# Tails of keys and queries loaded once per sequence, and the first sequence's query loads issued from ScalarE

## The chip, the cores and the metric

The kernel runs on one core of a Trainium2 chip. The metric is device time in microseconds; lower is better. The engines are named as in the profile: PE (TensorE, with PEld for its weight loads), DVE (VectorE), ACT (ScalarE), POOL (GpSimd) and SP (SyncE, which computes nothing here and issues DMAs). A row marked SPq or ACTq is the issue of a DMA on that engine's instruction stream.

## The reference, cut to what matters

Attention with a threshold over 4 sequences of 8 heads, 576 positions and 64 features, then two feed-forward layers on the result, all in float32:

```python
scores = q @ k^T / sqrt(64)                       # per sequence and head, 576 x 576
thresh = max(scores, -1) - tau
attn   = exp(where(scores >= thresh, scores, -1e9) - max)
attn   = attn / (sum(attn, -1) + 1e-9)
x      = (attn @ v) laid out as (4 * 576, 512)
x      = (h * clip(h + 3, 0, 6) / 6) @ w_out      # h = x @ w_in, 512 -> 2048 -> 512
x      = (max(h, 0) ** 2) @ w2_out                # h = x @ w2_in
```

## The kernel before, in words

A *unit* is a pair of heads of one sequence, so there are 16 units, 4 to a sequence (`u.b` is the sequence, `u.p` the pair, `u.i` the running number). 576 positions are 4 tiles of 128 (`NT = 4`) and a *tail* of 64. A unit has 9 *jobs*: 4 tiles of queries for each head and one job for the two tails together, so a sequence has 36 jobs. A job goes through the engines like this: `scores` on PE (name `s`), `soft1` and `soft2` on DVE, ACT and POOL (minimum `nm`, exponential, mask and sum, and a split into two halves of 16 bits, the last piece of which is line 281 on POOL, `gl` or `p`), then a transposing DMA issued by SP (line 283, `pt<-gl` in the first sequence, `pt<-p` later), and 5 jobs later (`LAG`) the product with the values on PE (`av`, line 305, name `o`). `finish` transposes a unit's result into `xh` and `xl`, the inputs of the first layer.

Before a unit's jobs, `prep_steps` transposes its keys and queries on PE (line 143, `tps`) and copies them on ACT. In the first sequence (`u.plain`) ACT alone copies; in later ones ACT and DVE split each value in two. The loads come two units ahead: in `run`, at a unit's jobs 2, 4 and 6 (`LOADS`), `load_qk` and `load_v` issue the loads for the unit after next. `kraw`, `qraw` and `vraw` have two buffers each. `load_qk` makes three DMAs for each of k and q: one for the four tiles, and one for each half of the partitions that brings the 64 tail rows of both heads of the pair.

The layers' weights come as 64-bit floats. Each of 64 weight tiles is loaded (`wd`, 512 KB), turned to 32 bits (lines 478 to 487, `wc` and `wraw`), split into two parts (lines 506 and 507) and written to DRAM (`scr`, line 490), from where the later sequences read it. Three `wd` tiles are in flight at most (`NWD`). The first tile is asked for after job 14 (`FIRST_W`). `hidden` (line 547, `hp`) and `output` (line 581, `y`) are the layers' matmuls; the steps of the next sequence's attention are put between them.

The order of instructions on each engine is not that of the code: a scheduler of the framework lists them by its own estimate of when each is ready. Each engine then runs its list strictly in order, and SP's list holds nearly all loads, all transposing DMAs and all writes.

Of the kernel before, what the change touches and what calls it, by code (L numbers as in the profile page):

```python
# [10 lines left out]
F32 = mybir.dt.float32  # L11
# [21 lines left out]
def attention_moe_moe_kernel(  # L33
# [12 lines left out]
    nc = tc.nc  # L46
    B, H, S, D = q.shape
    DM = out.shape[1]
    DFF = moe_w_in.shape[1]
    P = 128  # L50
    NT = S // P
    TAIL = S - NT * P
    assert TAIL * 2 == P and D * 2 == P
    NPAIR = H // 2
# [10 lines left out]
    ld = ctx.enter_context(tc.tile_pool(name="ld", bufs=1))  # L65
# [9 lines left out]
    ident = const.tile([P, P], F32, name="ident")  # L75
# [12 lines left out]
    own = [slice(0, D), slice(D, 2 * D)]  # L88
# [28 lines left out]
    class Unit:  # L117
        pass

    def load_qk(u, nm, eng=nc.sync):  # L120
        src = k if nm == "k" else q
        t = ld.tile([P, NT + 1, 2, D], F32, name=f"{nm}raw", bufs=2)
        pr = src[u.b, 2 * u.p:2 * u.p + 2]
        eng.dma_start(out=t[:, 0:NT], in_=pr[:, 0:NT * P, :].rearrange("h (p t) d -> p t h d", t=NT))

        for o in own:
            eng.dma_start(out=t[o, NT], in_=pr[:, NT * P:, :].rearrange("h p d -> p h d"))
        setattr(u, nm, t)

    def load_v(u):  # L130
        u.v = t = ld.tile([P, 2, NT + 1, D], F32, name="vraw", bufs=2)
        pr = v[u.b, 2 * u.p:2 * u.p + 2]
        nc.sync.dma_start(out=t[:, :, 0:NT, :], in_=pr[:, 0:NT * P, :].rearrange("h (p t) d -> p h t d", t=NT))
        for o in own:
            nc.sync.dma_start(out=t[o, :, NT, :], in_=pr[:, NT * P:, :].rearrange("h p d -> p h d"))

    def transpose_part(t, part, wide=False):
        if wide:
            a = ps_s.tile([P, 2, 512], F32, tag="s", name="tps")[:, 0]
        else:  # L140
            a = ps_a.tile([P, 512], F32, tag="acc", name="tps")
        for i, j in enumerate((0, 1) if part == 0 else (2, 3, 4)):
            nc.tensor.transpose(a[:, i * P:i * P + P], t[:, j].rearrange("p h d -> p (h d)"), ident)  # L143
        return a

    def cols(part):
        return (0, QA) if part == 0 else (QA, QB)

    def prep_steps(u):

        u.plain = u.b == 0
        if u.plain:

            u.qf = q_pl[:, u.i % 2]
            u.kf = xr[u.i % 2]
            for part in (0, 1):
                a = transpose_part(u.k, part, u.i == NPAIR)
                c0, n = cols(part)
                nc.scalar.activation(out=u.kf[:, c0:c0 + n], in_=a[:, 0:n], func=AF.Copy)
                yield  # L160
            for part in (0, 1):
                a = transpose_part(u.q, part, u.i == NPAIR)
                c0, n = cols(part)
                for h in range(2):
                    qf = u.qf[own[h], h * NT + 2 * part:h * NT + 2 * part + 2, :]
                    nc.scalar.activation(out=qf, in_=a[own[h], 0:2 * P].rearrange("p (t c) -> p t c", t=2), func=AF.Copy, scale=qs[own[h]])
                    if n > 2 * P:
                        nc.scalar.activation(out=u.qf[own[h], 2 * NT, own[h]], in_=a[own[h], 2 * P:n], func=AF.Copy, scale=qs[own[h]])
                yield
            yield from prep_v(u)  # L170
            return
        u.qs = [q_st[h][u.i % 2] for h in range(2)]
        u.ks = [k_st[h][u.i % 2] for h in range(2)]
        for part in (0, 1):
            a = transpose_part(u.k, part, u.i == NPAIR)
            c0, n = cols(part)
            for h in range(2):
                kh = u.ks[h][own[h], 0, c0:c0 + n]
                nc.scalar.activation(out=kh, in_=a[own[h], 0:n], func=AF.Copy)
                nc.vector.tensor_tensor(out=u.ks[h][own[h], 1, c0:c0 + n], in0=a[own[h], 0:n], in1=kh.bitcast(F32), op=ALU.subtract)  # L180
            yield
        for part in (0, 1):
            a = transpose_part(u.q, part, u.i == NPAIR)
            c0, n = cols(part)
            for h in range(2):
                for a0, d0, m in ((0, c0, 2 * P), (2 * P, NT * P + 64, n - 2 * P)):
                    if m > 0:
                        qh = u.qs[h][own[h], d0:d0 + m]
                        nc.scalar.activation(out=qh, in_=a[own[h], a0:a0 + m], func=AF.Copy, scale=qs[own[h]])
                        nc.vector.scalar_tensor_tensor(out=u.qs[h][own[1 - h], d0:d0 + m], in0=a[own[h], a0:a0 + m], scalar=qs[own[h]], in1=qh.bitcast(F32), op0=ALU.mult, op1=ALU.subtract)  # L190
            yield
        for h in range(2):
            nc.sync.dma_start(out=u.ks[h][own[1 - h], 0, :].bitcast(F32), in_=u.ks[h][own[h], 0, :].bitcast(F32))
        yield from prep_v(u)

    def prep_v(u):

        vin = u.v.rearrange("p h t d -> p (h t d)")
        am = st.tile([P, 1], F32, name="am", bufs=2)
        nc.vector.tensor_reduce(out=am, in_=vin, axis=AX.X, op=ALU.max, apply_absolute_value=True)  # L200
        a = ps_a.tile([P, 512], F32, tag="acc", name="vm")
        nc.tensor.matmul(a[:, 0:P], lhsT=am.to_broadcast([P, P]), rhs=ident, start=True, stop=True)
        u.vsc = sc = st.tile([P, 1], F32, name="vsc", bufs=2)
        nc.vector.tensor_reduce(out=sc, in_=a[:, 0:P], axis=AX.X, op=ALU.max)
        yield
        nc.vector.tensor_scalar(out=sc, in0=sc, scalar1=2.0 ** -100, scalar2=2.0 ** -13, op0=ALU.max, op1=ALU.mult)
        nc.vector.reciprocal(out=sc, in_=sc)
        nc.vector.tensor_scalar(out=sc.bitcast(I32), in0=sc.bitcast(I32), scalar1=0x7f800000, scalar2=None, op0=ALU.bitwise_and)
        v16 = at.tile([P, 2, 2, NT + 1, D], F16, name="v16")
        u.v1, u.v2 = v16[:, 0], v16[:, 1]  # L210
        v1 = u.v1.rearrange("p h t d -> p (h t d)")
        v2 = u.v2.rearrange("p h t d -> p (h t d)")
        if u.b < 2:
            nc.scalar.activation(out=v1, in_=vin, func=AF.Copy, scale=sc)
            nc.vector.scalar_tensor_tensor(out=v2, in0=vin, scalar=sc, in1=v1, op0=ALU.mult, op1=ALU.subtract)
        else:
            nc.scalar.activation(out=vin, in_=vin, func=AF.Copy, scale=sc)
            nc.scalar.activation(out=v1, in_=vin, func=AF.Copy)
            nc.gpsimd.tensor_tensor(out=v2, in0=vin, in1=v1, op=ALU.subtract)
# [152 lines left out]
    def run(us, all_jobs, pr):  # L372
        n = len(all_jobs)
        for i in range(n + LAG):
            if i < n:
                j = all_jobs[i]
                if j.first:
                    if pr is not None:
                        for _ in pr:
                            pass  # L380
                    pr = prep_steps(us[j.u.i + 1]) if j.u.i + 1 < len(us) else None
                scores(j)
                soft1(j)
            if i >= 1 and i - 1 < n:
                soft2(all_jobs[i - 1])
                jj = all_jobs[i - 1]
                if jj.hd == "t":
                    recips(jj.u, 2 * NT, 1)
                elif jj.t % 2:
                    recips(jj.u, jj.hd * NT + jj.t - 1, 2)  # L390
            x = i - LAG
            if 0 <= x < n:
                j = all_jobs[x]
                if j.hd == "t" or j.u.b == 0:
                    av([j])
                elif j.t % 2:
                    av([all_jobs[x - 1], j])
                if j.hd == 1 and j.t % 2:
                    finish(j.u, j.t // 2)
            if i < n and pr is not None:  # L400
                if next(pr, 1) == 1:
                    pr = None
            if i < n and all_jobs[i].u.i + 2 < len(us):
                nu = us[all_jobs[i].u.i + 2]
                if all_jobs[i].n == LOADS[0]:
                    load_qk(nu, "k")
                if all_jobs[i].n == LOADS[1]:
                    load_qk(nu, "q")
                if all_jobs[i].n == LOADS[2]:
                    load_v(nu)  # L410
            yield (i, n)
        return pr
# [285 lines left out]
```

## Time and profile before

| | us |
|---|---|
| three timed runs | 1114.97, 1115.55, 1117.37 (median 1115.55) |
| profiled execution | 1115.3, of which the span of the instructions is 1113.5 |
| PE busy | 1054.3 (95%) |
| ACT, DVE, POOL busy | 731.5, 721.4, 591.9 |
| share of the chain that ended last on PE | 68% |

The span is cut into stretches in the rows below. The first sequence's attention fills the first 100 us, the weight tiles are converted from 53.6 to 353.1 us, and after 400 us PE is busy nearly without a gap. Busy times of PE are modelled at their ends, so a busy PE may still be short of its peak.

### The profile page before, as it was taken

What the parts mean: (1) busy time and instruction counts of PE and PEld (TensorE: products, weight loads), DVE (VectorE), ACT (ScalarE), POOL (GpSimd) and SP (SyncE); (2) the same over time, 40 slices, a digit from 0 to 9 for tenths busy, and PEclk for the clock granted to TensorE, in tenths of its full rate; (3) what the DMA queues carried; (4) which work ended last, traced back from release to release, by engine and by line L of the source; (5) the groups of instructions that cost most, each with busy time, mean ns of one, the idle gap of its engine ahead of it and who ended that gap; (6) DMA issues with size and microseconds to landing.
All of it is one profiled execution on the core that took longest, in us unless ns stands there. A gap on an engine that the chain in (4) does not pass through costs nothing.

```text
span 1113.5 us, 24082 instructions
## 1 busy us (share of the span) xinstructions
PE 1054.3 (95%) x9136; PEld 1018.6 (91%) x9136; DVE 721.4 (65%) x1306; ACT 731.5 (66%) x1384; POOL 591.9 (53%) x654
## 2 busy tenths in 40 slices
PE   6777899999899999999999999999999999999998
PEld 4556789988888999999999999999999999999998
DVE  5798678887787756767666656767656343435342
ACT  6887778788787757667775657757765445435432
POOL 5786678878679744456544454445643232214221
PEclk9989999999999999999999999999999999999999
DMA  6898999999998565556754545446544243323221
GB/s 143 181 234 183 268 237 274 267 248 271 256 266 203 136 154 139 133 123 133 152 125 125 130 135 127 103 125 120 119 111 110 85 118 80 94 77 86 77 67 43
DMA packets 291267, 168.70 MB, mean 152 GB/s; under 512 B 223824, under 2 KB 252496, under 8 KB 291152
## 3 DMA queue, kind: packets, MB, share of 16 engines
q1 hardware_dynamic: 289824, 166.84, 61.5%
q8 instruction: 72, 1.18, 0.5%
q10 hardware_dynamic: 1328, 0.33, 0.1%
q14 instruction: 43, 0.35, 0.1%
HBM read 99.62 MB, written 21.50 MB: 109 GB/s over the span
## 4 chain that ended last, share of the span: by engine, by line
PE 68%; DVE 2%; ACT 2%; POOL 1%; DMA 1%; issue 1%; SPq 0%; DVEq 0%; POOLq 0%; ACTq 0%
PE y L581 30%; PE hp L547 28%; PE s L250 4%; PE o L305 3%; PE tps L143 1%; PE ot L608 1%; DMA wd<-in_moe_w_out_dram 0%; DMA wd<-in_moe_w_in_dram 0%; DVE wc L481 0%; PE xT L322 0%; DVE wraw L482 0%; POOL gl L561 0%; POOL xl L337 0%; DVE wraw L487 0%; DVE ya L587 0%
## 5 line engine op out<-in xcount | busy, mean ns | idle before, releaser
L561 POOL TENSOR_TENSOR gl<-g,gh 128x576 fp32r<-128x576 f32 x128 | 193.8, 1516 | 257.3 <-ACT gh L560 253.5
L581 PE MATMUL y<-gh,who 128*128 128x288 f32 x1024 | 225.3, 301 | 8.3 <-DVE e L273 4.7
L547 PE MATMUL hp<-xh,whi 128*128 128x288 f32 x1024 | 224.8, 301 | 7.4 <-DVE g L558 2.7
L581 PE MATMUL y<-gh,wlo 128*128 128x288 f32 x1024 | 220.6, 296 | 0.0
L581 PE MATMUL y<-gl,who 128*128 128x288 f32 x1024 | 219.0, 297 | 0.3 <-POOL gl L561 0.2
L547 PE MATMUL hp<-xh,wli 128*128 128x288 f32 x1024 | 219.0, 296 | 0.0
L547 PE MATMUL hp<-xl,whi 128*128 128x288 f32 x1024 | 218.7, 295 | 0.0
L581 PEld LDWEIGHTS y<-gh,who 128*128 128x128 f32 x1024 | 163.9, 189 | 10.3 <-issue 2.7
L547 PEld LDWEIGHTS hp<-xh,whi 128*128 128x128 f32 x1024 | 163.6, 189 | 9.3 <-DVE e L273 2.4
L581 PEld LDWEIGHTS y<-gh,wlo 128*128 128x128 f32 x1024 | 164.9, 189 | 0.0
L547 PEld LDWEIGHTS hp<-xh,wli 128*128 128x128 f32 x1024 | 164.8, 189 | 0.0
L547 PEld LDWEIGHTS hp<-xl,whi 128*128 128x128 f32 x1024 | 164.6, 189 | 0.0
L581 PEld LDWEIGHTS y<-gl,who 128*128 128x128 f32 x1024 | 163.8, 189 | 0.7 <-POOL gl L561 0.7
L256 DVE TENSOR_REDUCE nm<-s 128x1 f32<-128x576 f32 x144 | 107.9, 751 | 36.8 <-PE s L250 29.1
L281 POOL TENSOR_TENSOR p<-e,p 128x512 f16<-128x512 f32 x108 | 130.8, 1211 | 0.0
L587 DVE TENSOR_TENSOR ya<-y,ya 128x576 f32<-128x576 f32 (+1 forms) x97 | 71.6, 748 | 77.2 <-PE y L581 76.6
L506 ACT ACTIVATE who<-wraw 128x512 fp32r<-128x512 f32 x128 | 79.4, 628 | 63.2 <-PE y L581 37.5
L273 DVE SCALAR_TENSOR_TENSOR e<-s,thr,e 128x576 f32<-128x576 f32 x108 | 88.0, 815 | 42.0 <-ACT e L266 41.3
L305 PE MATMUL o<-v,pt 128*128 128x64 f16 (+1 forms) x2016 | 93.0, 198 | 17.7 <-DMA pt<-gl 10.9
L507 DVE TENSOR_TENSOR wlo<-wraw,who 128x512 fp32r<-128x512 f32 x96 | 80.5, 846 | 43.4 <-ACT who L506 41.1
L305 PEld LDWEIGHTS <-pt 128*128 128x128 f16 x2016 | 74.6, 99 | 33.2 <-DMA pt<-gl 13.9
L279 ACT ACTIVATE p<-e 128x576 f16<-128x576 f32 x108 | 73.4, 680 | 36.7 <-DVE e L273 35.2
(92 smaller groups left out, 1700.5 us busy)
## 6 DMA issues: line engine op xcount, KB each, us to landing
wraw<-scr SPq DMA_DIRECT2D x192, 256.0 KB, 2.7
wd<-in_moe_w_in_dram SPq DMA_DIRECT2D x32, 512.0 KB, 5.0
scr<-wraw SPq DMA_DIRECT2D x64, 256.0 KB, 4.0
wd<-in_moe_w_out_dram SPq DMA_DIRECT2D x32, 512.0 KB, 5.5
kraw<-in_k_dram SPq DMA_DIRECT2D x16, 256.0 KB, 4.1
vraw<-in_v_dram SPq DMA_DIRECT2D x16, 256.0 KB, 3.3
out_dram<-wd SPq DMA_DIRECT2D x16, 256.0 KB, 2.8
qraw<-in_q_dram SPq DMA_DIRECT2D x15, 256.0 KB, 3.8
```

The lines of the kernel that those rows point to most:

```text
L250: nc.tensor.matmul(s[:, half, 0:HALF], lhsT=u.qs[sl][:, cs], rhs=u.ks[sl][:, kk, c], start=i == 0, stop=i == len(ops) - 1)
L256: nc.vector.tensor_reduce(out=j.nm, in_=j.s, axis=AX.XY, op=ALU.min)
L273: nc.vector.scalar_tensor_tensor(out=j.e, in0=j.s, scalar=j.thr, in1=j.e, op0=ALU.is_le, op1=ALU.mult, accum_out=u.sm[:, col:col + 1])
L279: nc.scalar.activation(out=p16[:, 0:S], in_=e, func=AF.Copy)
L281: nc.gpsimd.tensor_tensor(out=p16[:, S + TAIL:], in0=e[:, 0:NT * P], in1=p16[:, 0:NT * P], op=ALU.subtract)
L305: nc.tensor.matmul(o[:, n * w:n * w + w], lhsT=j.pt[:, c, :], rhs=vv[:, hs, vc, :], start=i == 0, stop=i == len(ops) - 1)
L506: nc.scalar.activation(out=h, in_=t, func=AF.Copy)
L507: (nc.gpsimd if fresh else nc.vector).tensor_tensor(out=l, in0=t, in1=h.bitcast(F32), op=ALU.subtract)
L547: nc.tensor.matmul(hp[:, a, 0:HALF], lhsT=w[:, cs], rhs=x[c][:, a * HALF:(a + 1) * HALF], start=i == 0, stop=i == 3 * NC - 1)
L561: nc.gpsimd.tensor_tensor(out=gl, in0=gf, in1=gh.bitcast(F32), op=ALU.subtract)
L581: nc.tensor.matmul(a[:, k_, 0:HALF], lhsT=w_hl[wuse[(tag, "o", f)]][w][:, cs], rhs=g[f][:, k_ * HALF:(k_ + 1) * HALF], start=i == 0, stop= ...
L587: nc.vector.tensor_tensor(out=y, in0=av_, in1=y, op=ALU.add)
```

## The change

`load_qk` no longer loads tails. A new function, `load_tails`, loads the tails of all 8 heads of a sequence into one tile (`ktail`, `qtail`, one buffer each) with two DMAs, one for each half of the partitions. It is called when the first unit of a sequence is loaded. `transpose_part` takes the fifth 128-column piece from that tile instead of from `kraw` or `qraw`, which shrink from five tiles to four. And in `run`, as long as the job at hand belongs to the first sequence, the queries of the unit after next are loaded through ACT's queue.

```diff
+    def load_tails(b, nm, eng=nc.sync):
+        t = ld.tile([P, H, D], F32, name=f"{nm}tail", bufs=1)
+        for o in own:
+            eng.dma_start(out=t[o], in_=(k if nm == "k" else q)[b, :, NT * P:, :].rearrange("h p d -> p h d"))
+        tails[nm] = t
+
+    tails = {}
+
     def load_qk(u, nm, eng=nc.sync):
         src = k if nm == "k" else q
-        t = ld.tile([P, NT + 1, 2, D], F32, name=f"{nm}raw", bufs=2)
+        t = ld.tile([P, NT, 2, D], F32, name=f"{nm}raw", bufs=2)
         pr = src[u.b, 2 * u.p:2 * u.p + 2]
-        eng.dma_start(out=t[:, 0:NT], in_=pr[:, 0:NT * P, :].rearrange("h (p t) d -> p t h d", t=NT))
-
-        for o in own:
-            eng.dma_start(out=t[o, NT], in_=pr[:, NT * P:, :].rearrange("h p d -> p h d"))
+        eng.dma_start(out=t, in_=pr[:, 0:NT * P, :].rearrange("h (p t) d -> p t h d", t=NT))
+        if u.p == 0:
+            load_tails(u.b, nm, eng)
         setattr(u, nm, t)
+        setattr(u, nm + "t", tails[nm])
...
-            nc.tensor.transpose(a[:, i * P:i * P + P], t[:, j].rearrange("p h d -> p (h d)"), ident)
+            x = tail[:, 2 * u.p:2 * u.p + 2] if j == NT else t[:, j]
+            nc.tensor.transpose(a[:, i * P:i * P + P], x.rearrange("p h d -> p (h d)"), ident)
...
+                eng = nc.scalar if all_jobs[i].u.b == 0 else nc.sync
                 if all_jobs[i].n == LOADS[0]:
                     load_qk(nu, "k")
                 if all_jobs[i].n == LOADS[1]:
-                    load_qk(nu, "q")
+                    load_qk(nu, "q", eng)
```

With other loads to place, the scheduler lists the rest anew as well. Three places follow; line numbers in the changed kernel are 12 to 14 higher behind the new function, so that 295 there is the transposing DMA of line 283 here.

On SP, where the first weight tiles are loaded. Before, this is behind the thirteenth transposing DMA of the kernel (the second row here):

```order
L127 DMA qraw<-in_q_dram 64x2x64 x2
L283 DMA_TRANSPOSE pt<-gl 128x9x128
L463 DMA wd<-in_moe_w_in_dram 128x4x256 x3
L283 DMA_TRANSPOSE pt<-gl 128x9x128 x2
L490 DMA scr_681<-wraw 128x512
L463 DMA wd<-in_moe_w_in_dram 128x4x256
L133 DMA vraw<-in_v_dram 128x2x256
L135 DMA vraw<-in_v_dram 64x2x64 x2
```

In the changed kernel it is ahead of the first transposing DMA:

```order
L134 DMA kraw<-in_k_dram 128x8x64
L477 DMA wd<-in_moe_w_in_dram 128x4x256 x3
L134 DMA kraw<-in_k_dram 128x8x64
L295 DMA_TRANSPOSE pt<-gl 128x9x128 x5
L143 DMA vraw<-in_v_dram 128x2x256
L145 DMA vraw<-in_v_dram 64x2x64
```

So the first three weight loads moved from behind 13 transposing DMAs to ahead of all of them, and the write of the first converted tile (`scr`), which stood ahead of the sixteenth, now stands behind the sixth.

On SP, at the end of the first sequence. Before, all 36 of its transposing DMAs (the last five are in the third and sixth row) come ahead of the next `w_out` tiles:

```order
L124 DMA qraw<-in_q_dram 128x8x64
L127 DMA qraw<-in_q_dram 64x2x64 x2
L283 DMA_TRANSPOSE pt<-gl 128x9x128 x2
L133 DMA vraw<-in_v_dram 128x2x256
L135 DMA vraw<-in_v_dram 64x2x64 x2
L283 DMA_TRANSPOSE pt<-gl 128x9x128 x3
L490 DMA scr_1757<-wraw 128x512
L465 DMA wd<-in_moe_w_out_dram 128x1024
L283 DMA_TRANSPOSE pt<-p_1810 128x9x128
L490 DMA scr_1829<-wraw 128x512
L465 DMA wd<-in_moe_w_out_dram 128x1024
```

In the changed kernel:

```order
L295 DMA_TRANSPOSE pt<-gl 128x9x128 x2
L479 DMA wd<-in_moe_w_out_dram 128x1024
L504 DMA scr_1817<-wraw 128x512
L479 DMA wd<-in_moe_w_out_dram 128x1024
L134 DMA kraw<-in_k_dram 128x8x64
L504 DMA scr_1891<-wraw 128x512
L479 DMA wd<-in_moe_w_out_dram 128x1024
L134 DMA qraw<-in_q_dram 128x8x64
L295 DMA_TRANSPOSE pt<-gl 128x9x128 x5
```

Three weight loads, two writes and the loads of a later unit's keys and queries moved ahead of the last five transposing DMAs of the first sequence.

On ACT, during the jobs of the first sequence's third unit, where the fourth unit's queries are copied (`ya`) and the second unit's result is written (`xh_104`). Before:

```order
L266 ACTIVATE gh<-s,nm 128x576
L166 ACTIVATE ya<-tps,qs 64x256
L329 ACTIVATE xh_104<-xT 64x64
L168 ACTIVATE ya<-tps,qs 64x64
L166 ACTIVATE ya<-tps,qs 64x256
L279 ACTIVATE gl<-gh 128x576
```

In the changed kernel:

```order
L278 ACTIVATE gh<-s,nm 128x576
L324 ACTIVATE os<-o,sm 128x64
L291 ACTIVATE gl<-gh 128x576
L341 ACTIVATE xh_104<-xT 64x64
L134 DMA qraw<-in_q_dram 128x8x64
L178 ACTIVATE ya<-tps,qs 64x256
L180 ACTIVATE ya<-tps,qs 64x64
L125 DMA qtail<-in_q_dram 64x8x64 x2
```

The load of a coming unit's queries stands directly ahead of two of those copies, and the two query tail loads of the second sequence follow them; none of the three stood on ACT before.

## Rows read from the trace of the kernel before

**Rows 1.** Busy time and instructions of each engine by stretch, granted clock, DMA share, GB/s.

```profile
0.00:10.00 10.00, 4.03 (x13) 2.91 (x14) 1.31 (x5) 4.02 (x9) 5.78 (x22) 1.00 0.60 143
10.00:60.00 50.00, 37.53 (x310) 27.95 (x309) 40.63 (x97) 40.47 (x82) 34.27 (x68) 0.95 0.82 171
60.00:100.00 40.00, 30.95 (x306) 22.99 (x304) 36.69 (x86) 36.38 (x81) 33.05 (x58) 0.93 0.99 218
100.00:110.00 10.00, 8.39 (x102) 7.91 (x100) 6.80 (x16) 6.90 (x16) 6.75 (x10) 1.00 0.86 172
110.00:120.00 10.00, 5.61 (x70) 5.02 (x71) 3.34 (x10) 4.06 (x11) 2.48 (x4) 0.99 1.06 251
120.00:400.00 280.00, 260.81 (x2258) 251.72 (x2257) 220.50 (x379) 225.96 (x433) 217.34 (x202) 0.99 0.94 238
400.00:1113.00 713.00, 706.99 (x6087) 700.12 (x6085) 412.15 (x718) 413.72 (x756) 292.28 (x293) 1.00 0.46 111
```

**Rows 2.** Waits of PE from 10 to 100 us: total, times, longest.

```profile
PE o L305 <- DMA pt<-gl: 8.4, 5, 3.9
```

**Rows 3.** Timeline of SP's issues: start, duration, instructions.

```profile
49.23 1.68 SPq L463 DMA_DIRECT2D wd<-in_moe_w_in_dram  x3
51.11 5.51 SPq L283 DMA_TRANSPOSE pt<-gl  x2
57.60 0.35 SPq L490 DMA_DIRECT2D scr<-wraw  x1
...
60.52 1.61 SPq L283 DMA_TRANSPOSE pt<-gl  x1
...
64.78 7.82 SPq L283 DMA_TRANSPOSE pt<-gl  x4
```

**Rows 4.** Timeline of POOL: the last pieces of jobs 16 and 18.

```profile
51.84 1.17 POOL L281 TENSOR_TENSOR gl<-gh,gl 128x512 f16<-128x512 f32 x1
...
55.88 1.15 POOL L281 TENSOR_TENSOR gl<-gh,gl 128x512 f16<-128x512 f32 x1
```

**Rows 5.** Timeline of PE; in brackets the idle time before, and its end.

```profile
58.37 1.67 PE L305 MATMUL o<-v,pt 128*128 128x128 f16 x14 [3.92 <-DMA pt<-gl]
```

**Rows 6.** Timeline: DMA issues of queries and tails on ACT, of tails on SP.

```profile
0.74 0.71 ACTq L124 DMA_DIRECT2D qraw<-in_q_dram  x1
1.49 1.38 ACTq L127 DMA_DIRECT2D qraw<-in_q_dram  x2
...
73.34 1.35 SPq L127 DMA_DIRECT2D kraw<-in_k_dram  x2
```

**Rows 7.** Timeline of the start: tail transpose on PE, then DVE.

```profile
6.87 0.42 PE L143 MATMUL tps<-ident,kraw 128*128 128x128 f32 x1
...
8.00 0.82 DVE L200 TENSOR_REDUCE am<-vraw 128x1 f32<-128x640 f32 x1 [0.87 <-DMA vraw<-in_v_dram]
...
10.81 0.76 DVE L256 TENSOR_REDUCE nm<-s 128x1 f32<-128x576 f32 x1 [1.99 <-PE s L246]
```

**Rows 8.** Timeline of ACT past 60 us: weight conversions (first, last) and a split.

```profile
62.82 0.66 ACT L478 ACTIVATE wc<-wd 128x512 f32<-128x512 f32 x1
63.38 0.62 ACT L506 ACTIVATE whi<-wraw 128x512 fp32r<-128x512 f32 x1
...
69.64 0.68 ACT L478 ACTIVATE wc<-wd 128x512 f32<-128x512 f32 x1 [0.37 <-DMA wd<-in_moe_w_out_dram]
```

**Rows 9.** Timeline of all engines where the first sequence ends.

```profile
106.38 4.66 SPq L283 DMA_TRANSPOSE pt<-gl  x3
...
111.03 0.58 PE L305 MATMUL o<-v,pt 128*128 128x64 f16 x14 [2.43 <-DMA pt<-gl]
...
111.73 0.45 SPq L465 DMA_DIRECT2D wd<-in_moe_w_out_dram  x1
...
116.63 0.66 ACT L478 ACTIVATE wc<-wd 128x512 f32<-128x512 f32 x1 [1.84 <-DMA wd<-in_moe_w_out_dram]
```

**Rows 10.** DMA issues: count, KB each, median us from issue to landing.

```profile
wd<-in_moe_w_out_dram SPq DMA_DIRECT2D x32, 512.0 KB, 5.5
```

More of the change, by code (lines that the diff above doesn't have):

```diff
@@ L135, in load_v, with transpose_part @@
             nc.sync.dma_start(out=t[o, :, NT, :], in_=pr[:, NT * P:, :].rearrange("h p d -> p h d"))
-    def transpose_part(t, part, wide=False):
+    def transpose_part(u, nm, part, wide=False):
+        t, tail = getattr(u, nm), getattr(u, nm + "t")
         if wide:
@@ L156, in prep_steps @@
             for part in (0, 1):
-                a = transpose_part(u.k, part, u.i == NPAIR)
+                a = transpose_part(u, "k", part, u.i == NPAIR)
                 c0, n = cols(part)
@@ L161, in prep_steps @@
             for part in (0, 1):
-                a = transpose_part(u.q, part, u.i == NPAIR)
+                a = transpose_part(u, "q", part, u.i == NPAIR)
                 c0, n = cols(part)
@@ L174, in prep_steps @@
         for part in (0, 1):
-            a = transpose_part(u.k, part, u.i == NPAIR)
+            a = transpose_part(u, "k", part, u.i == NPAIR)
             c0, n = cols(part)
@@ L182, in prep_steps @@
         for part in (0, 1):
-            a = transpose_part(u.q, part, u.i == NPAIR)
+            a = transpose_part(u, "q", part, u.i == NPAIR)
             c0, n = cols(part)
```

## The prediction

> **What bounds the kernel now.** I read the stretches first [rows 1]. From 400 us on PE is busy 706.99 of 713 us: nothing that SP or ACT do there can matter. From 120 to 400 it is idle 19.2 of 280. What is left lies in front: PE's idle time is 12.5 us from 10 to 60, 9.1 from 60 to 100, 6.0 from 100 to 120. So the time after 120 us is a block of PE work that moves as a whole, and the question is when the first sequence's attention hands it over. In that attention PE is not the bound: from 60 to 100 us DVE is busy 36.69 and ACT 36.38 of 40 us, but from 10 to 60 only 40.63 and 40.47 of 50, so 9.4 and 9.5 us are idle there, and from 100 to 120 they do 10.1 and 11.0 us of work in 20 [rows 1].
>
> Why there is idle time in the middle I read from PE's waits: between 10 and 100 us it stood 8.4 us before value products for a transposed tile [rows 2]. The largest of these, 3.92 us, ends at 58.37 [rows 5]. SP's issues say where it is from [rows 3]: three weight loads of 512 KB go out at 49.23, then two transposing DMAs take 5.51 us to issue, where three take 4.66 at 106.38 [rows 9], then SP waits for the first converted weight tile, which it has to write at 57.60. Only then, at 60.52, goes the transposing DMA of job 16, whose data POOL had finished at 51.84 + 1.17 = 53.01 [rows 4]. It is 7.5 us late. Those of jobs 17 and 18 come after 64.78, and job 18's data were ready at 55.88 + 1.15 = 57.03: at least 7.7 us late. These DMAs waited for SP's order, not for their data.
>
> **The change, part by part.**
>
> *Start.* The four tail DMAs in front carry 512 KB in all instead of 128 KB, so 393,216 more bytes lie ahead of the first values and the next keys. At the first stretch's 143 GB/s that is 2.7 us [rows 1]; it is the upper end. The lower is 0: the first values' reduction on DVE ends at 8.82, and DVE then idles 1.99 us until the first scores [rows 7]; the key tail is transposed at 6.87 [rows 7], behind other transposes. The tails are the nearer of the two, since the first scores need them whole. I take +1.0.
>
> *SP.* Before, it issues twelve key tails (two for each of units 0 to 5), ten query tails and five query loads during the first sequence; now four key tails and one query load. That is 22 issues less; at 1.35/2 = 0.68 us each [rows 6] 14.9 us of SP's time. None of it counts by itself; it counts where a transposing DMA stands behind it. What the scheduler makes of the room counts more: the three weight loads go ahead of the first transposing DMA instead of behind the thirteenth, and the first converted tile's write stands behind the sixth, with the conversion on DVE's list ahead of that job's own mask. So the pile-up at 49 to 66 us is gone. I count the wait of 3.92 [rows 5] as saved: −3.9. Upper end 0: the first value products, which follow three 512 KB loads instead, may wait as long. Lower end −9.4, all of DVE's idle time from 10 to 60 [rows 1]. I stay with the one wait, because the first product comes five jobs behind its DMA and has slack that a product in mid-stream has not.
>
> *ACT.* Four query loads and two tail loads are new on its list; an issue there takes 0.71 and 1.38/2 = 0.69 us [rows 6], 4.1 us in all, during which ACT computes nothing. Do they also wait? Each stands ahead of copies that wait for the very transposes that free its buffer, so no. Queued behind each are those copies, then the next job's exponential, for which DVE waits. By their places, two of the four query loads come in the first 20 us and one before 60, where ACT has 9.5 us to spare; the rest, one query load and two tails, fall where ACT is busy 91%: 3 × 0.69 = +2.1. Against that, three conversions and two splits of weights that ran on ACT from 62.8 to 70 us now come earlier: 3 × 0.66 + 2 × 0.62 = 3.2 us [rows 8]. Together −1.1; ends −3.2 (the issues all hidden) and +4.1 (no slack used).
>
> The page "DMA: Bandwidth & Descriptors" of the Trainium skill says (section "Issuing engines are not separate DMA queues") that DMAs from several engines run on the same 16 DMA engines and only the issuing sequencer's time is saved. By it the move to ACT's queue brings no bandwidth and is worth 0 unless SP's order holds something up; the pile-up above says it does, so I weigh it as a rival below.
>
> *End of the first sequence.* Now PE waits 2.43 us for a transposed tile at 111.03, ACT 1.84 us for the next `w_out` tile at 116.63, since that was issued only at 111.73, behind the transposing DMAs of 106.38 [rows 9]. In the changed order three such tiles go ahead of the last five transposing DMAs. I count ACT's wait as gone and PE's as left: −1.8. The lower end is −6.0, all of PE's idle time there; the upper is the slow rival below.
>
> *Later.* In the later sequences' loads 40 tail issues become 8, and the PE's transposes read as many columns as before, from another tile. From 120 to 400 us PE idles 19.2 us for many reasons [rows 1]; the new order may win or lose some of it. The one-buffer tails must wait for the last unit's transposes, which stand on PE about where SP comes to them. I take 0, from −4 to +4, a fifth of that idle time.
>
> *Sum.* 1.0 − 3.9 − 1.1 − 1.8 = −5.8. The profiled execution took 1115.3 us (span 1113.5 and 1.8 around it), which is the median of the timed runs, 1115.55, but for 0.25. So 1115.3 − 5.8 = **1109.5**.
>
> **The rivals.**
>
> *Slower: the weights get in front of the last transposes.* Ahead of the first sequence's last five transposing DMAs stand three weight loads, two writes and two loads: 3 × 512 + 4 × 256 KB = 2.62 MB, which at the 251 GB/s of 110 to 120 us is 10.4 us of transfers [rows 1]. On PE, 40 matmuls stand between the last scores of the sequence and the first of these five products; at 706.99/6087 = 0.116 us each [rows 1] they cover 4.6 us, and 5.8 are left. Besides, on ACT the conversion of the first of these weight tiles now stands ahead of the last three jobs' exponentials: if it waits for the whole landing, 5.5 us [rows 10], they do too. That is +11.3, and with the terms ahead of it (+1.0 − 3.9 − 1.1) 1115.3 + 7.3 = 1122.6. It decides from the point where those transposes land 4 us or more later than PE comes to them, which takes up what the middle won. For it speaks that two transposing DMAs took 5.51 us to issue behind three such loads [rows 3]; against it, that the five become ready one after the other, 2.8 us apart (36 jobs in the first 100 us), so that only the first ones meet the full queue, and that the same bytes then no longer hold up the conversions that follow.
>
> *No change: SP's lateness is cover.* The transposed tiles are used five jobs later, and DVE and ACT are busy 92% from 60 to 100 us; if they are the true bound, what is gained before 60 us is spent waiting later, and the new issues on ACT eat the rest. Time 1115.3, the sum with all terms 0. For it: of the 8.4 us that PE waited, all is before an engine that is itself not the bound. Against it: DVE and ACT idle 9.4 us just there. The rule of the Trainium skill named above leads to this case too.
>
> *More: the hand-over comes earlier and everything keeps pace.* If all of the idle time from 10 to 60 on DVE goes and PE's 6.0 from 100 to 120 too: 1115.3 + 1.0 − 9.4 − 1.1 − 6.0 = 1099.8.
>
> **How the numbers follow.** A measurement of this kernel can tell about 0.2%, 2.2 us, from no change. Forecast (1104 to 1113): 0.52. More, below 1104: 0.12. No change (1113.3 to 1117.8): 0.17. Slower, the first rival or a smaller share of it: 0.19, of which about 0.09 above 1120. The likeliest is the forecast, 1109.5. With 0.07 left below 1102 and 0.09 above 1120 the range is 1102 to 1120; the forecast's own range is 1104 to 1113. Faster by over 0.2%: 0.64; same 0.17; slower 0.19.
>
> **What the profile will show.** If the steps hold: PE has no wait of 3 us or more for a transposed tile between 40 and 70 us; the transposing DMAs of jobs 16 to 18 go within 2 us of their data; DVE and ACT are busier from 20 to 50 us and less from 60 to 100; the queries' issues on ACT take 0.7 us each with no wait ahead; PE is busy over 15 of the 20 us from 100 to 120; and past 400 us nothing differs but the shift. The start is wrong if the first scores come over 2 us later. The prediction fails if the last five transposed tiles of the first sequence, or the first ones behind the early weight loads, hold PE for 4 us or more, or if the shift at 120 us is lost again by 400.

## The result, and the profile after

The changed kernel takes 1129.63 us (median of 4, 1129.14 to 1130.04) against 1115.38 for the kernel before on the same chip: ratio 1.0119, 95% interval 1.0094 to 1.0144. It is 14 us slower, outside the range given. Its profiled execution took 1129.9 us, with a span of 1128.0.

The stretches of [rows 1] in the changed kernel (busy time and instructions of PE, PEld, DVE, ACT, POOL; granted clock; DMA share; GB/s), the last one up to its end:

```profile
0.00:10.00 10.00, 3.56 (x12) 2.38 (x13) 1.31 (x5) 2.92 (x5) 5.77 (x22) 1.00 0.83 187
10.00:60.00 50.00, 36.54 (x272) 26.21 (x271) 44.04 (x94) 40.91 (x84) 36.93 (x64) 0.90 0.93 208
60.00:100.00 40.00, 30.83 (x337) 24.27 (x333) 32.37 (x78) 31.78 (x75) 27.15 (x52) 0.91 0.93 182
100.00:120.00 20.00, 14.45 (x135) 12.13 (x132) 14.95 (x33) 13.50 (x28) 13.68 (x21) 0.91 1.02 212
120.00:400.00 280.00, 253.57 (x2213) 244.35 (x2213) 212.94 (x369) 219.85 (x427) 207.35 (x198) 0.98 0.88 230
400.00:1128.00 728.00, 720.27 (x6185) 712.94 (x6183) 420.26 (x731) 420.65 (x769) 300.34 (x300) 1.00 0.46 111
```

From 10 to 60 us DVE does 44.04 us of work instead of 40.63, as forecast; from 60 to 100 it does 4.3 us less and ACT 4.6. But PE, which did 260.81 us of work from 120 to 400, now does 253.57. Over the span PE is busy 1059.2 us with the same 9136 matmuls (1054.3 before), and idle 1128.0 − 1059.2 = 68.8 instead of 59.2. So of the 14.5 us of span 9.6 are idle time of PE and 4.9 are matmuls that ran longer; the granted clock is 0.986 over the span against 0.992.

Four checkpoints, read from the timelines, say where the time went: the minimum of job 28 on DVE (the first of the sequence's last unit) and of job 36 (its last job), and the first and the 32nd finished hidden tile (`gh<-g` on ACT; the 32nd is the last of the first sequence's second layer). From there to the last hidden tile both kernels take 707.7 to 707.9 us.

| us | job 28 | job 36 | first hidden tile | 32nd hidden tile | between the tiles |
|---|---|---|---|---|---|
| before | 76.7 | 98.4 | 126.6 | 387.7 | 261.1 |
| changed | 76.1 | 108.8 | 134.3 | 402.0 | 267.7 |
| difference | −0.6 | +10.4 | +7.7 | +14.3 | +6.6 |

At job 28 nothing is lost. 8.3 us are lost from there to the first hidden tile and 6.6 in the 260 us after it. Of the 6.6, 3.8 are idle time of PE (21.8 us between the two tiles against 18.0) and 2.8 matmuls that ran longer (245.8 us busy against 243.1).

What PE waits for between 10 and 100 us in the changed kernel (total, times, longest); it answers to [rows 2]:

```profile
PE s L258 <- DVE gh L285: 12.2, 7, 3.0
...
PE o L317 <- DMA pt<-gl: 1.1, 1, 1.1
```

The waits of scores for masks before:

```profile
PE s L246 <- DVE gh L273: 4.3, 4, 2.0
```

The 8.4 us of waits for transposed tiles are down to 1.1; scores wait for DVE's masks instead, 12.2 us against 4.3. DVE between 25 and 33 us (start, duration; in brackets, in later rows, the idle time before):

```profile
25.39 1.37 DVE L495 TENSOR_SCALAR wc<-wc 128x512 int32<-128x512 int32 x1
26.68 0.81 DVE L285 SCALAR_TENSOR_TENSOR gh<-s,thr,gh 128x576 f32<-128x576 f32 x1
...
27.83 1.64 DVE L496 SCALAR_TENSOR_TENSOR wraw<-wd,wc 128x512 int32<-128x512 int32 x1
...
31.20 0.74 DVE L268 TENSOR_REDUCE nm<-s 128x1 f32<-128x576 f32 x1
...
32.60 1.72 DVE L496 SCALAR_TENSOR_TENSOR wraw<-wd,wc 128x512 int32<-128x512 int32 x1
```

Conversions of the early weight tiles stand between the first masks and minima. Job 10's minimum comes at 34.9 us instead of 30.5; by job 28 that is made up.

SP does what the order said: three weight loads ahead of the first transposing DMAs, and the sequence's last five behind three more, issued from 101.48 us on. These rows answer to [rows 3, 9]:

```profile
10.99 2.39 SPq L477 DMA_DIRECT2D wd<-in_moe_w_in_dram  x3
...
17.88 12.82 SPq L295 DMA_TRANSPOSE pt<-gl  x5
...
106.78 12.85 SPq L295 DMA_TRANSPOSE pt<-gl  x5
```

Around 82 us, on DVE and on PE:

```profile
82.03 0.82 DVE L212 TENSOR_REDUCE am<-vraw 128x1 f32<-128x640 f32 x1 [3.29 <-DMA vraw<-in_v_dram]
...
83.73 2.26 PE L258 MATMUL s<-xr,ya 128*128 128x288 f32 x4 [3.04 <-DVE gh L285]
```

`am<-vraw` is the reduction of the values of the *second* sequence's first unit. It stands ahead of the masks of jobs 27 to 31 of the *first*, and they wait with it. At the sequence's end DVE, ACT and PE show the same thing with weights (DVE's rows first, then ACT, DVE, PE):

```profile
106.14 1.69 DVE L227 SCALAR_TENSOR_TENSOR v<-vraw,vsc,v 128x640 f16<-128x640 f32 x1
...
110.16 0.68 DVE L496 SCALAR_TENSOR_TENSOR wraw<-wd,wc 128x512 int32<-128x512 int32 x1
...
111.50 1.42 DVE L495 TENSOR_SCALAR wc<-wc 128x512 int32<-128x512 int32 x1
...
124.77 0.66 ACT L492 ACTIVATE wc<-wd 128x512 f32<-128x512 f32 x1 [2.20 <-DMA wd<-in_moe_w_in_dram]
...
125.97 0.62 ACT L341 ACTIVATE xh<-xT 64x64 fp32r<-64x64 f32 x2
...
127.77 0.41 DVE L342 TENSOR_TENSOR xl<-xT,xh 128x256 fp32r<-128x256 f32 x1
...
126.58 0.41 PE L155 MATMUL tps<-ident,kraw 128*128 128x128 f32 x2 [1.78 <-DVE xl L342]
```

A value split of the second sequence (1.69) and two conversions stand ahead of and among the last three masks, and the last results `xh`, `xl`, which the first layer needs, come behind a conversion that waits 2.20 us for its load.

### The profile page after: what moved, and what is told of

The parts are those of the page before. It is cut to its first block, busy times and chain, and to the rows that moved or that the text cites. A ratio compares the mean times of both kernels' runs of the same rounds, so it can differ in the third digit from the quotient of the medians.

```text
span 1128.0 us, 24031 instructions
## 1 busy us (share of the span) xinstructions
PE 1059.2 (94%) x9136; PEld 1022.3 (91%) x9136; DVE 725.9 (64%) x1306; ACT 729.6 (65%) x1384; POOL 591.2 (52%) x654
## 4 chain that ended last, share of the span: by engine, by line
PE 72%; DVE 8%; ACT 7%; DMA 7%; issue 3%; POOL 2%; SPq 1%; DVEq 0%; ACTq 0%; POOLq 0%
PE y L595 31%; PE hp L561 29%; PE s L262 4%; PE o L317 4%; DMA wd<-in_moe_w_in_dram 3%; DMA wd<-in_moe_w_out_dram 2%; PE s L258 2%; DVE wraw L496 1%; DVE nm L268 1%; DMA vraw<-in_v_dram 1%; ACT wc L492 1%; DVE gh L285 1%; PE tps L155 1%; DVE wraw L501 1%; PE ot L622 1%
## 5 line engine op out<-in xcount | busy, mean ns | idle before, releaser
L561 PEld LDWEIGHTS hp<-xh,whi 128*128 128x128 f32 x1024 | 164.1, 190 | 12.2 <-issue 6.3
L317 PEld LDWEIGHTS <-pt 128*128 128x128 f16 x2016 | 76.8, 100 | 27.0 <-issue 9.5
```

Source lines behind the costliest of these rows:

```text
L317: nc.tensor.matmul(o[:, n * w:n * w + w], lhsT=j.pt[:, c, :], rhs=vv[:, hs, vc, :], start=i == 0, stop=i == len(ops) - 1)
L561: nc.tensor.matmul(hp[:, a, 0:HALF], lhsT=w[:, cs], rhs=x[c][:, a * HALF:(a + 1) * HALF], start=i == 0, stop=i == 3 * NC - 1)
```

## The experiments

Behind each kernel stands its ratio to the kernel before, run on the same chip, with the 95% interval; 1.001 is 1.1 us. No edit changes what is computed. The gates below add a dependence by one more small operation on POOL, whose output is overwritten; but with each the scheduler lists everything anew, so that no edit moves one instruction alone.

**Halves of the change, and the early weights.** Three theories at first: E, the early conversions of the first weight tiles cost the time; A, the query issues on ACT do; T, the bulk of tails does. `e1_tails_only` puts the query loads back on SP:

```diff
-                    load_qk(nu, "q", eng)
+                    load_qk(nu, "q")
```

> The changed kernel with all query loads back on SP; the tails still come once per sequence. Theory E (early weights: the first three conversions stand on DVE and ACT among the masks of the first jobs, where DVE has no room): here too the first conversion stands behind the fourth mask, so the minimum of job 10 comes 4 us or more later than before's 30.5 us, and the time is 1121 to 1130. Theory A (the query issues on ACT cost the time): 1114 to 1118. Theory T (the tails of a whole sequence are a burst of 512 KB that makes later loads land late): 1121 or more, but with the delay at the values' reduction of the fourth unit, not at job 10.

`e2_act_only` is the kernel before with the other half:

```diff
+                eng = nc.scalar if all_jobs[i].u.b == 0 else nc.sync
-                    load_qk(nu, "q")
+                    load_qk(nu, "q", eng)
```

> The kernel before with the coming units' queries (with their tails, per pair) issued from ACT in the first sequence; nothing else. Here the first conversion stands behind the fifteenth mask on DVE. Theory E: job 10's minimum within 2 us of before, time 1112 to 1119. Theory A: the issues on ACT (12 DMAs at 0.7 us) hold its exponentials up: 1119 to 1125. Theory T: no bulk of tails here, time as before, 1115.

`e3_after_gate14` is the changed kernel, where a one-column write from job 14's minimum into the first three `wd` tiles holds their loads back:

```diff
         nc.vector.tensor_reduce(out=j.nm, in_=j.s, axis=AX.XY, op=ALU.min)
+        if j.u.i * 9 + j.n == 13:
+            gate_nm.append(j.nm)
...
         d = wt.tile([P, 512, 2], I32, name="wd", bufs=NWD)
+        if i < NWD:
+            nc.gpsimd.tensor_tensor(out=d[:, 0, 0:1].bitcast(F32), in0=gate_nm[0], in1=tau_a, op=ALU.add)
```

> The changed kernel with the first three weight loads made to wait for job 14's minimum (a one-column write to each of the tiles), so that the first conversion stands behind the sixteenth mask on DVE, and most of the last transposing DMAs stand ahead of the weight loads. Theory E: job 10's minimum at 30 to 32 us instead of 34.9, and the first layer matmul within 3 us of before's 99.9; time 1113 to 1121. Theory T and theory A: the time stays 1124 to 1130, since the bulk of tails and the issues on ACT are as in the changed kernel.

`e4_before_early` is the kernel before with its weights early (`FIRST_W = 4` for 14).

> The kernel before with the first weight tile asked for after job 4 instead of 14 (one number); tails and query loads as before. The first conversion now stands behind the fifth mask on DVE, as in the changed kernel. Theory E: job 10's minimum 4 us or more later than before, the first layer matmul 4 to 10 us later than 99.9, time 1119 to 1128. Theories T and A: 1113 to 1118, since neither tails nor query issues differ from before.

| | ratio, interval | job 10 | job 28 | job 36 | first hidden | 32nd hidden |
|---|---|---|---|---|---|---|
| before | | 30.5 | 76.7 | 98.4 | 126.6 | 387.7 |
| changed | 1.0119 | 34.9 | 76.1 | 108.8 | 134.3 | 402.0 |
| e1 | 1.0016, 1.0000 to 1.0032 | 34.9 | 79.5 | 101.9 | 123.3 | 390.0 |
| e2 | 1.0008, 0.9996 to 1.0020 | 30.1 | 74.8 | 100.1 | 122.3 | 389.7 |
| e3 | 1.0007, 0.9991 to 1.0023 | 32.6 | 76.8 | 104.8 | 131.7 | 391.7 |
| e4 | 1.0009, 0.9995 to 1.0023 | 35.5 | 80.4 | 104.5 | 127.4 | 386.8 |

E falls as a cause by itself, though e3 came where it put it: in e1 and e4 job 10 is 4.4 and 5.0 us late, as in the changed kernel, and the time is that of before within 0.2%. A and T fall: either half alone costs 0.1 to 0.2%, and e3, which has both, 0.07%. Neither half gains anything. The 14 us come with both together, and go with a gate on three loads, so they are not a cost of the loads by themselves but of the list that the scheduler made of them. And three things did not fit the prediction's picture: in e4 jobs 28 and 36 come 3.7 and 6.1 us later than before and the first hidden tile under 1; in e1 and e2 the first hidden tile comes 3.3 and 4.3 us *earlier* than before and the end does not; in e3 it comes 5.1 later and 1.1 are left.

**What stands ahead of the first sequence's last jobs.** These are DVE's lists from mask 26 to mask 38. A number is a job's mask, M the reduction of a unit's values and V a value split, k and q the key and query splits of the second sequence, x a result of the first, [w6] a weight conversion:

```
before  26 x 27 28 k x k k 29 k V q 30 q M 31 q q 32 q x 33 q x x x 34 35 36 V 37 M 38
changed 26 M 27 28 x V k k k k 29 q 30 x q 31 x q x q x M q 32 33 q V 34 [w6] 35 36 [w7] 37 38
e5      26 27 28 x V k k 29 k k [w6] q 30 q x 31 M q x q x x 32 q 33 q M 34 V 35 36 [w7] 37 38
e6      26 M 27 28 x V k k k k 29 q 30 x q 31 x q x q x M q 32 33 q V 34 35 36 M 37 x 38
e7      26 27 28 x V k k 29 k k q 30 q M 31 x q x q 32 x x 33 q q M 34 35 V 36 37 [w6] x 38
```

In the changed kernel the second sequence's first two reductions stand 4 and 6 masks earlier, its first value split 3, and two weights ahead of 35 and 37. Between the minima of jobs 28 and 36 DVE does 57 instructions, 24.00 us, in 32.6 us; before 48, 19.73 us, in 21.7. So 4.3 us of the 10.9 are more work and 6.7 are waits. Three theories: V, the wait for that load at 82 us; Y, the weights at the end; S, neither, the loss is made past 120 us. The changed kernel was run once more, as `e0_after`, beside `e5_after_am` (the reduction M held back to job 31), `e6_after_w6` (weight tiles 6 to 8 held back to job 37) and `e7_both`:

```diff
         am = st.tile([P, 1], F32, name="am", bufs=2)
+        if u.i == 4:
+            nc.gpsimd.tensor_tensor(out=am, in0=gate[31], in1=tau_a, op=ALU.add)
...
         d = wt.tile([P, 512, 2], I32, name="wd", bufs=NWD)
+        if 6 <= i < 9:
+            nc.gpsimd.tensor_tensor(out=d[:, 0, 0:1].bitcast(F32), in0=gate[37], in1=tau_a, op=ALU.add)
```

> The changed kernel once more, as it is, for a second measure on the chip of the next three. All theories: 1127 to 1131.

> The changed kernel with the reduction of the second sequence's first values held back on DVE until the minimum of job 31 is there, where it stands in the code; before, it stood ahead of the masks of jobs 27 to 31 and waited 3.29 us for its load, issued at 75.54 and landed at 82.0. Theory V (that load is late and DVE's list stops behind it): the wait of 3.0 us on PE at 83.73 goes, job 31's minimum comes 4 to 6 us earlier than 92.8, time 1120 to 1125. Theory Y (the w_out tiles ahead of the sequence's last jobs cost the time): 1126 to 1130. Theory S (neither; the loss is made past 120 us): 1126 to 1130 even if the hand-over comes earlier.

> The changed kernel with weight tiles 6 to 8 made to wait for job 37's minimum, so that the last five transposing DMAs of the first sequence stand ahead of these loads and the conversions behind mask 38 instead of 34; the wait at 82 us stays. Theory Y: the first layer matmul 3 to 5 us earlier than 110.4, time 1122 to 1126. Theory V: job 31's minimum as late as in the changed kernel (92 to 93), time 1126 to 1130. Theory S: 1126 to 1130.

> The changed kernel with both edits: the values' reduction held back to job 31, weight tiles 6 to 8 to job 36. Theories V and Y together: the first layer matmul at 99 to 104 us and the time 1114 to 1120. V alone: 1120 to 1125, as with its edit alone. Y alone: 1122 to 1126. Theory S: 1126 to 1130.

| | ratio, interval | job 31 | job 36 | first hidden | 32nd hidden | between |
|---|---|---|---|---|---|---|
| e0 | 1.0124, 1.0100 to 1.0147 | 90.7 | 107.4 | 132.9 | 403.9 | 271.1 |
| e5 | 1.0050, 1.0030 to 1.0069 | 91.3 | 106.1 | 128.4 | 393.5 | 265.1 |
| e6 | 1.0089, 1.0069 to 1.0110 | 90.4 | 106.9 | 131.1 | 397.4 | 266.3 |
| e7 | 1.0031, 1.0013 to 1.0048 | 88.7 | 103.9 | 127.0 | 389.8 | 262.8 |

One reduction moved back gives 9.2 us (1129.15 to 1119.95), three loads held back 4.3, both 11.1. The time of e6 is in Y's range. S falls as it was put, since the times moved; but of the 10.4 us by which the 32nd tile comes earlier in e5 than in e0 only 4.5 are there at the first, and of the 6.5 of e6 only 1.7: the larger part is made past 120 us. V falls as it was put: job 31 comes no earlier in e5 than in e0, and in the second profile of the changed kernel the load was nearly there, for the same time:

```profile
80.33 0.82 DVE L212 TENSOR_REDUCE am<-vraw 128x1 f32<-128x640 f32 x1 [1.33 <-DMA vraw<-in_v_dram]
```

So it is not that one wait. That it is where the second sequence's preparation and the weights stand is theory P. Four more kernels, with the same two gates, test it.

> The changed kernel with the values' reductions of the second sequence's first and second unit held back to the minima of jobs 31 and 36, and weight tiles 6 to 8 to job 37, so that on DVE they stand where they stood before the change (behind masks 30, 36 and 38). The first three weight tiles stay early, the loads as in the change. Theory P (what costs is the second sequence's preparation and the w_out conversions listed ahead of the first sequence's last jobs): first layer matmul at 100 to 104 us, time 1114 to 1118. Theory Q (the early first three weights, the tails or the issues on ACT still cost by themselves): 1118 to 1124.

> The changed kernel with only the second sequence's second unit's reduction held back to job 36 (from behind mask 31 to behind mask 35). Theory P: a part of the loss goes, time 1123 to 1127, with job 31's minimum as late as in the changed kernel (90 to 93 us), since the first unit's reduction stays early. Theory V (the first unit's late load alone is what costs): 1127 to 1131.

> The changed kernel with all of it held back: the first three weight tiles to job 14, the two reductions to jobs 31 and 36, weight tiles 6 to 8 to job 37. On DVE and SP the order is then nearly that of before, with the change's loads. Theory P and the prediction's gain together: the loads' change is worth something once the order is the old one, time 1109 to 1114. Theory N (the change of loads is worth nothing by itself): 1114 to 1118.

> The changed kernel with only the two reductions held back, to jobs 31 and 36; the weights are where the scheduler puts them. Theory P: less than the first unit's reduction alone (1119.95): 1116 to 1120, with the rest up to before from the weight tiles. Theory V: the same as with the first unit's alone, 1119 to 1121.

| | ratio, interval | job 36 | first hidden | 32nd hidden | between |
|---|---|---|---|---|---|
| e8 | 1.0074, 1.0049 to 1.0099 | 103.4 | 125.9 | 396.3 | 270.4 |
| e9 | 1.0089, 1.0068 to 1.0111 | 106.3 | 135.0 | 399.4 | 264.4 |
| e10 | 1.0047, 1.0024 to 1.0070 | 102.4 | 128.3 | 394.1 | 265.8 |
| e11 | 1.0048, 1.0031 to 1.0065 | 105.2 | 128.8 | 394.0 | 265.2 |

Half right. With the two reductions and these weights held back (e8) the hand-over is where it was before, 125.9 against 126.6: the 8.3 us go with those three edits. But the time is 8 us above before, in Q's range and not in P's, because the stretch between the tiles takes 270.4. e9 came as P said; e11 came as V said: holding back the second reduction as well adds nothing to the first alone (e5). e10, nearly the old order with the new loads, came above the ranges of both theories and above before, so the predicted gain does not show there either.

**The converse, and the rest.** `e12_before_am_first` is the kernel before, with job 28's threshold waiting for M (which is emitted at job 27 there; `am` and `vsc` get a third buffer): DVE's list is the old one up to mask 27 and then reads "k x k V k k M 28". `e13_gate8` and `e14_gate12` are e3 with job 8 and 12; at the end of the sequence their lists are close to that of before ("29 k q M 30 ... 35 V 36 M 37 x 38" in e13; in e14 the V stands behind 33). L is that the change's loads cost the time by themselves.

```diff
+        if j.u.i * 9 + j.n + 1 == 28:
+            nc.gpsimd.tensor_tensor(out=j.thr, in0=am4(), in1=tau_a, op=ALU.add)
```

> The kernel before, where job 28's threshold is made to wait for the values' reduction of the second sequence's first unit, so that four key splits, one value split and this reduction stand on DVE ahead of mask 28; up to mask 27 and in all loads it is the kernel before. Theory P (the second sequence's preparation ahead of the first one's last jobs is what costs): job 31's minimum 3 to 8 us later than 86.6, first finished hidden tile 3 to 8 us later than 125.4, time 1118 to 1124. Theory L (it is the change's loads, by their bytes or queues): 1113 to 1117.

> The changed kernel with the first three weight loads held back to job 8's minimum (where the run with 14 gave 1116.0). The end of the first sequence is then listed as before: first reduction of the second sequence behind mask 29, the second behind 36, w_out tiles behind 38, the last five transposing DMAs ahead of their loads. Theory P: 1112 to 1118, first finished hidden tile 121 to 127. If the predicted gains from SP's order are real once the listing is kept: 1108 to 1112. Theory L: 1122 or more.

> The same with job 12 instead of 8; the end of the first sequence is listed in the same way. Theory P: 1112 to 1118. Predicted gains: 1108 to 1112. Theory L: 1122 or more.

> The kernel before once more, for a second profile: all theories 1113 to 1117, and the stretch from the first finished hidden tile to the thirty-seventh within 3 us of 266.2.

| | ratio, interval | job 31 | job 36 | first hidden | 32nd hidden | between |
|---|---|---|---|---|---|---|
| e12 | 1.0052, 1.0036 to 1.0069 | 90.4 | 102.4 | 126.3 | 391.4 | 265.1 |
| e13 | 1.0034, 1.0014 to 1.0054 | 86.3 | 99.1 | 120.1 | 391.4 | 271.4 |
| e14 | 1.0057, 1.0037 to 1.0077 | 86.4 | 97.1 | 122.9 | 393.8 | 270.9 |
| b0 | one run, 1114.65 us | 87.2 | 99.0 | 127.4 | 387.4 | 260.0 |

e12 costs 6.5 us by the medians (1121.05 against 1114.5) with the same loads as before, as P said, with job 31 3.8 us late; but at the first hidden tile (126.6 before, by the mark of the tables), where P had 3 to 8 us, nothing of it is left, and the loss is in the stretch behind. e13 and e14, at 1119.3 and 1121.1, miss the ranges of P, of the predicted gains and of L. e13 is the sharpest: its hand-over is 6.5 us *earlier* than before and its end 4.8 us later (median 1119.32 against 1114.5). There PE waits for the second sequence's masks; from 119 to 400 us, first the changed order (e13), then before:

```profile
PE hp L567 <- DVE e L289: 7.0, 4, 3.4
PE y L601 <- DVE e L289: 4.5, 3, 1.8
```

```profile
PE y L581 <- DVE e L273: 3.4, 5, 1.1
...
PE hp L547 <- DVE e L273: 2.6, 3, 1.0
```

These waits are the smaller part of it. Between the first and the 32nd hidden tile (columns as in the stretches above), in e13, before and in e12:

```profile
120.05:391.42 271.37, 250.37 (x2149) 242.50 (x2150) 214.19 (x362) 216.30 (x419) 205.99 (x195) 0.96 0.88 235
126.56:387.68 261.12, 243.08 (x2141) 234.96 (x2140) 210.62 (x362) 215.99 (x417) 207.80 (x195) 0.99 0.96 243
126.28:391.41 265.13, 243.40 (x2146) 235.52 (x2145) 207.98 (x361) 216.18 (x418) 206.57 (x195) 0.99 0.96 243
```

Of the 10.3 us that e13 takes longer than before, 3.0 are idle time of PE (21.0 against 18.0) and 7.3 are nearly the same matmuls that ran longer, at a granted clock of 0.96 instead of 0.99. In e12 the 4.0 us are nearly all idle time.

Two profiles of one kernel differ by 1.1 us in this stretch (before, b0) and by 3.4 (changed, e0); the kernels differ by 11. So that spread is real, but what in the list sets the waits and the clock there was not found: it goes neither with the place of the first reduction (behind mask 30 in e7 and e8, which take 262.8 and 270.4) nor with the loads (e3 and e13 have the same ones, 260.0 and 271.4). That stays open. Over the changed kernel and e1 to e14 the place of the first M tells only the slowest apart: behind mask 26 (changed, e6, e9) the medians are 1124.3 to 1129.6 us, behind a later one 1116.0 to 1123.3, and within that group it does not order them.

## Why the prediction was wrong

**Start, +1.0: right.** The first minimum comes at 11.52 us, against 10.81 [rows 7]: +0.7.

**SP's pile-up, −3.9, and ACT, −1.1: the events came, the gain did not.** Waits for transposed tiles fell from 8.4 [rows 2] to 1.1 us, the DMAs of jobs 16 to 18 go 2.8, 1.4 and 1.0 us behind their data, and ACT's query issues take 0.61 to 0.72 us with no wait. (Job 16's 2.8 is past the 2 us that was to be seen.) But the data of these jobs come later: job 16's last piece starts at 58.0 us, against 51.84 [rows 4], behind the early conversions; in e1 and e4, which have them too, it starts at 58.6 and 56.2, in e2 and e3, which do not, at 52.2 and 51.2. The working priced the converted tiles on ACT and never on DVE, where the first three cost 6 instructions of 0.41 to 1.72 us just where PE needs masks. It took DVE's idle time of 10 to 60 us as room; from 20 to 40 us, where it did 15.93 us of work before, DVE has 0.6 us left. At job 28 the three terms together are worth −0.6 instead of −4.0. That is the rival "SP's lateness is cover", and e1 and e2 bear it out for this part: between 10 and 100 us their waits for transposed tiles are 1.1 and 3.3 us, and their times are within 0.2% of before. The page "DMA: Bandwidth & Descriptors" of the Trainium skill (section "Issuing engines are not separate DMA queues") says that issuing from several engines saves only the sequencer's time; e2 agrees, at +0.1%.

The price of the issues on ACT was also too high. The working took ACT to compute nothing meanwhile, but an exponential runs beside the issue at 50.49 for all of its 0.61 us:

```profile
50.41 0.74 ACT L278 ACTIVATE gh<-s,nm 128x576 f32<-128x576 f32 x1 [0.33 <-DVE nm L268]
50.49 0.61 ACTq L134 DMA_DIRECT2D qraw<-in_q_dram  x1
```

**End of the first sequence, −1.8: this step failed, at +8.3.** It read the new order at three places only, where loads and conversions had moved, and took the rest of the lists as unmoved. The scheduler had listed everything anew: the second sequence's reductions stand 4 and 6 masks earlier. The slow rival had the right place and half of the mechanism. The transposing DMAs themselves were not late (those of jobs 34 and 36 were issued within 0.2 us of their data), but the conversions did stand ahead of the last masks and results, and e6 gives 4.3 us at the end for holding these loads back. The reduction M, for which e5 gives 9.2 at the end, is a cause that no rival had. At the first hidden tile e5 and e6 have 4.5 and 1.7 us of it, and e8, with both reductions and these loads held back, all 8.3. From 100 to 120 us PE is busy 14.45 us, where over 15 was to be seen.

**Later, 0 within ±4: +6.6.** What failed is the sentence on which the sum stands, that the work after 120 us "is a block of PE work that moves as a whole". From 400 us on it does (707.7 and 707.9). Before that it does not: first hidden tiles 3.3 to 6.5 us earlier (e1, e2, e13, e14) went with 32nd ones 2.0 to 6.1 us later, and one 5.1 later (e3) with a 32nd tile 4.0 later and 1 us in the timed runs. PE interleaves the first layers with the second sequence's attention there, and from 120 to 400 us it idles between 18.7 (e4) and 26.8 us (e0) according to the list; before it was 19.2 and 18.0 (b0).

**Range.** The sum had four terms for what the scheduler was seen to move and none for what it may move unseen; and it counted idle time alone, while 4.9 of the 14.5 us of span are matmuls that ran longer. Fifteen kernels with other lists, the changed one and e1 to e14, have medians from 1116.0 to 1129.6 us; none beat the kernel before.

## What to carry to other kernels

Where a scheduler makes the lists, price the list and not the edit: compare every engine's whole list, and look first for work of the next phase that now stands ahead of this phase's last instructions, and what it waits for. A gain at the front of a phase whose engines are 90% busy is worth nothing until it is seen at the checkpoint where the phase ends, and one there nothing until the next phase takes it over. Here fifteen other lists were no better than the old one, so in such a kernel an edit that removes a small, visible wait should be forecast around no change with a long tail on the slow side, unless the rest of the order can be held as it was.

## What the hardware showed

The second operation of a weight conversion, which reads two tiles from SBUF, takes 0.69 us alone (median of 6) and 1.21 us (median of 31, up to 1.90) where a GpSimd tensor operation runs beside it; 0.68 and 1.20 in the kernel before. A mask, with one operand in PSUM, takes 0.82 us alone and 0.81 beside one. All 37 of this form in the changed kernel (shortest, median, longest in ns), and the masks of the later sequences:

```profile
L496 DVE SCALAR_TENSOR_TENSOR wraw<-wd,wc x37: 670/991/1903, 24.7 to 388.7; 128x512 int32<-128x512 int32 x37
```

```profile
L285 DVE SCALAR_TENSOR_TENSOR e<-s,thr,e x108: 797/818/819, 116.8 to 871.0; 128x576 f32<-128x576 f32 x108
```

The Trainium skill says this on the page "SBUF — State Buffer" (section "Who interferes with whom"): a DVE instruction with two SBUF inputs contends with a GpSimd instruction that reads SBUF, one with at most one, outside its 2-port modes, does not. The trace agrees: 1.21 us against 0.69 for the first, no difference for the second. So a conversion that is moved among the jobs, where POOL is busy, can cost 1.75 times what it costs alone.

Idle time of PE is not the whole loss; the granted clock differs too. In the changed kernel, from 10 to 60, 60 to 100 and 100 to 120 us it is 0.90, 0.91 and 0.91, where [rows 1] have 0.95, 0.93 and 0.99 to 1.00. It is lowest in these two stretches, the columns as above:

```profile
20.00:30.00 10.00, 6.46 (x31) 4.27 (x31) 9.59 (x21) 9.03 (x16) 7.92 (x12) 0.69 0.68 135
80.00:90.00 10.00, 6.84 (x79) 5.96 (x79) 6.42 (x13) 5.95 (x15) 5.17 (x8) 0.66 0.93 176
```

A mean of 0.66 to 0.69 is about two thirds of the stretch at the lower of the two levels, 1.2 GHz. In both PE was idle over 3 us of 10, the second time with the wait of 3.04 us shown above. Over the kernels run, the same 9136 matmuls are busy from 1053.9 us (e12, clock 0.991 over the span) to 1061.9 (e0, 0.984). The clock does not simply follow the idle time: up to 400 us PE idles 57.0 us in e12 at a mean of 0.98, and 52.1 in e10 at 0.95.
